# Loading the first batch's q and v by casting transfers from GpSimd's queue

## The chip, the cores and the metric

The kernel runs on one core of one Trainium2 chip. The metric is device time in microseconds (us) of that core, as the median over runs. The engines are named as in the profile: PE (TensorE matmul), PEld (its weight loads), DVE (VectorE), ACT (ScalarE), POOL (GpSimd) and SP (SyncE, which here only issues DMAs).

## What is computed

Four batches, eight heads, 768 tokens, head size 64. The first half is a recurrent retention; the second half mixes its output by a two-dimensional Fourier transform, normalises it and runs a two-layer ReLU network with a residual. Inputs and output are float32.

```python
state = gamma[None, :, None, None] * state + np.einsum('bhd,bhe->bhde', k[:, :, t], v[:, :, t])
y[:, :, t] = scale * np.einsum('bhd,bhde->bhe', q[:, :, t], state)
...
X = np.fft.fft(x, axis=1)
X = np.fft.fft(X, axis=2)
mixed = np.real(X).astype(np.float32)
u = x + mixed
...
ch = np.maximum(un @ w_ch1, 0.0) @ w_ch2
return (u + ch).astype(np.float32)
```

Here `gamma` is one decay per head, `x` is y with the heads side by side (512 wide), and `un` is `u` after its mean and variance are taken out. `w_ch1` is 512 x 2048, `w_ch2` 2048 x 512.

## The kernel before

The recurrence is done in chunks. The 768 tokens are six chunks of 128, and the heads are taken two at a time: four pairs i = 0 to 3, in the order of `PAIR_ORDER`. For each pair the kernel loads q, k and v as float32, casts them to float16 (k with its decay factor, giving `kd`), transposes q and kd on PE, multiplies them chunk by chunk (`wkA`), applies the decay mask on DVE (`atm`), forms the chunk states `wkK` from kd and v, scans them over the chunks on DVE, and adds the part inside a chunk (`atm` times v) and the part from earlier chunks (qT times state) in PSUM (`wkY`). ACT scales the result into the tile `x`. The Fourier transform follows as matmuls with cosine and sine tables (`csp`, `ssp`, `cd`, `sd`) that the kernel itself computes at the start on DVE (`ts_dve`, `td_dve`, lines 288 to 292) and ACT (`t_act`). Then come the two layers (`psh`, line 936 and, for the first half of batch 0, line 953; `psc`, line 979), with the weights cast to float16 by DMAs from POOL (`w1_unit`, line 993, and `w2_unit`, line 1000).

Batch 0 has units of its own, and its order is written out by hand in `first_units`; the function `pin` makes each engine keep exactly the order in which the units issue their instructions. Later batches are merged with the matmuls of the batch before by the times in `LD0`, `TS0` and the like.

These are the units that matter here, all for pair i of batch 0:

- `load_unit(0, i)` issues three loads from SP (line 165), q, k, v for two heads at once, 384 KB each, into buffers of the pool `inp`, which has 11. For q a partition holds six neighbouring tokens (`(p c)`), so a run in memory is 1536 bytes; for k and v it holds every 128th token (`(c p)`), with runs of 256 bytes.
- `q0_unit` (line 398) casts q on POOL into one of two tiles `q16z`, so that pair 2 has to wait until pair 0's was read.
- `k0_unit` (lines 407, 410) casts k on POOL, one instruction per head; for pair 3 ACT does the second head (line 414).
- `v0_unit` (line 423) casts v on POOL into one of four tiles; for pair 3 DVE does half of it (line 427).
- `t0_unit` transposes q (part 0) or kd (part 1) on PE (line 439), and `te_unit` copies the result out of PSUM on ACT (lines 447, 450).
- `am_unit` (line 464) multiplies, `ae_unit` (line 471) masks on DVE, `kv0_unit` (line 486) forms the states, `sc_unit` (line 495) scans, `yi_unit` and `yx_unit` (lines 510, 526) form y, `x0_unit` (line 539) scales it.
- `filler` (line 151) issues matmuls on zeros that nobody reads.
- `half_ids` (lines 351, 353) is two small POOL instructions between the second and the third pair.

On POOL these units stand behind the constants of the start (lines 198 to 347). Batch 1's loads from SP wait for the last but one w2 DMA (`load_unit(1, i, 6)`) and for a matmul of the first layer.

Of the kernel before, what the change touches and what calls it, by code (L numbers as in the profile page):

```python
# [12 lines left out]
ALU = mybir.AluOpType  # L13
f32 = mybir.dt.float32
f16 = mybir.dt.float16
# [3 lines left out]
P = 128  # L19
# [3 lines left out]
NCH = S // P  # L23
# [13 lines left out]
LD0, LD1 = (0.172, 0.226), (-0.370, 0.140)  # L37
HT0 = (0.655, 0.675, 0.673, 0.628)
NPE = 2
ACT_ROWS = ((2, 5, 6, 7, 8, 9, 10, 14), (0, 3, 6, 7, 9, 10, 11, 12, 14, 15), (2, 4, 5, 6, 7, 8, 10, 14))  # L40


@with_exitstack
def kernel(
# [13 lines left out]
    def pool(name, bufs, **kw):  # L58
        return ctx.enter_context(tc.tile_pool(name=name, bufs=bufs, **kw))

    const = pool("const", 1)
    inp = pool("inp", 11)
    vp = pool("vp", 4)
    kp = pool("kp", 3)
    tp = pool("tp", 2)
# [82 lines left out]
    def filler(n):  # L148
        def run():
            for _ in range(n):  # L150
                nc.tensor.matmul(wps, wz[:, 0:P], wz, start=True, stop=True)  # L151
        return run
# [5 lines left out]
    def load_unit(b, i, after=None):  # L158
        def run():
            h0 = 2 * PAIR_ORDER[i]  # L160
            for name, src in srcs.items():
                t = inp.tile([P, 2, NCH, D], f32, tag="in32", name=f"{name}32")
                rows = "h (p c) d -> p h c d" if b < NPE and name == "q" else \
                    "h (c p) d -> p h c d"
                dma = nc.sync.dma_start(t, src[b, h0:h0 + 2].rearrange(rows, p=P))  # L165
                if after is not None:
                    for x in (w_dma[after].ins, lb[0]["mm"].ins):
                        tc.add_manual_dep(dma.ins, x.name,
                                          mybir.DependencyInfo(mybir.DependencyClass.Sync,
                                                               mybir.DependencyReason.DATA),  # L170
                                          reason="loads in turn")
                if b > 1:
                    tc.add_manual_dep(dma.ins, a_of[b - 1, 1].ins.name,
                                      mybir.DependencyInfo(mybir.DependencyClass.Sync,
                                                           mybir.DependencyReason.DATA),
                                      reason="loads behind the transposes")
                in_of[name, b, i] = t
        return run

    for i in range(4):  # L180
        load_unit(0, i)()


    icol_i = const.tile([P, 8], i32, tag="icol_i")
# [44 lines left out]
    def gk_unit(hp):  # L229
        def run():  # L230
            nc.scalar.copy(gk5[:, hp, :, 1:], gk2[:, hp:hp + 1].unsqueeze(1).to_broadcast(
                [P, D, NCH - 2]))
        return run
# [62 lines left out]
    def ts_dve(c):  # L296
        return trig_dve(c, S, KN, icol[:, c:c + 1], icoln[:, c:c + 1])
# [10 lines left out]
    def t_act(idx, part):  # L308
        w = KN if idx < 3 else 257
        r = rs[2 * idx][:, 0:w]  # L310
        ra = rs[2 * idx + 1][:, 0:w]
        sc = float(2.0 * np.pi / (S if idx < 3 else DM))

        def run():
            if part == 0:
                nc.scalar.activation(ra, r, AF.Abs, bias=0.0, scale=1.0)
            elif idx < 3:
                src = (ra, r)[part - 1].rearrange("p (i t) -> p t i", t=2)
                dst = (csp, ssp)[part - 1]
                nc.scalar.activation(dst[:, :, idx, :], src, AF.Sin,  # L320
                                     bias=hpi if part == 1 else 0.0,
                                     scale=-sc if part == 1 else sc)
            else:
                src, dst = (ra, r)[part - 1], (cd16, sd16)[part - 1]
                nc.scalar.activation(dst[:, idx - 3, :], src, AF.Sin,
                                     bias=hpi if part == 1 else 0.0, scale=-sc)
        return run
# [65 lines left out]

    def q0_unit(i):
        def run():
            q16 = q16_of[0, i] = qzs[i % 2].rearrange("p h c d -> p (h c d)")[
                :, 0:NCH * P].rearrange("p (c h d) -> p c h d", c=NCH, h=2)
            nc.gpsimd.tensor_scalar(out=q16, in0=in_of.pop(("q", 0, i)).rearrange(
                "p h c d -> p c h d"), scalar1=1.0, scalar2=1.0, op0=ALU.mult, op1=ALU.mult)
        return run  # L400

    def k0_unit(i):
# [14 lines left out]

    def v0_unit(i):
        def run():
            v32 = in_of.pop(("v", 0, i)).rearrange("p h c d -> p c h d")  # L420
            v16 = v16_of[0, i] = vp.tile([P, NCH, 2, D], f16, tag="v16", name="v16")
            n = NCH if i < 3 else 3
            last_cast[0, i] = nc.gpsimd.tensor_scalar(
                out=v16[:, 0:n], in0=v32[:, 0:n], scalar1=1.0, scalar2=1.0, op0=ALU.mult,
                op1=ALU.mult)
            if n < NCH:
                nc.vector.tensor_copy(v16[:, n:], v32[:, n:])
        return run

    def t0_unit(i, part):  # L430
# [606 lines left out]
    def first_units():  # L1037
        def a(i):
            un = [am_unit(i, 0), am_unit(i, 1)]
            return un  # L1040

        def e(i, *hh):
            return [ae_unit(i, half, h2) for half, h2 in hh]

        def y(i):
            return [yi_unit(i, 0), yi_unit(i, 1)]

        def x(i):
            return [x0_unit(i, 0), x0_unit(i, 1)]

        std = ((0, 0), (0, 1), (1, 0), (1, 1))
        heads = ((0, 0), (1, 0), (0, 1), (1, 1))
        o = PAIR_ORDER
        un = [ts_dve(0), gk_unit(o[0]), gk_unit(o[1]), t_act(0, 0), t_act(0, 1),
              q0_unit(0), t0_unit(0, 0), filler(4), ts_dve(1), te_unit(0, 0), t_act(0, 2),
              k0_unit(0), t0_unit(0, 1), filler(3), te_unit(0, 1), ts_dve(2), td_dve(0), t_act(1, 0),
              t_act(1, 1), t_act(1, 2), v0_unit(0)]
        un += a(0) + [filler(1), kv0_unit(0)] + e(0, *std) + [sc_unit(0)]
        un += [q0_unit(1), t0_unit(1, 0), te_unit(1, 0), t_act(2, 0), t_act(2, 1), filler(4),
               k0_unit(1), t0_unit(1, 1), te_unit(1, 1)]  # L1060
        un += y(0) + [parity_consts, yx_unit(0), filler(2)] + x(0) + [t_act(2, 2), v0_unit(1),
                                                                     half_ids]
        un += a(1) + [csn_unit(0), filler(1), kv0_unit(1)] + e(1, *std) + [sc_unit(1)]
        un += [q0_unit(2), t0_unit(2, 0), te_unit(2, 0), csn_unit(1), filler(3), k0_unit(2),
               t0_unit(2, 1), te_unit(2, 1)]
        un += y(1) + [td_dve(1), yx_unit(1), filler(2)] + x(1) + [
            gk_unit(o[2]), t_act(3, 0), t_act(3, 1), v0_unit(2)]
        un += a(2) + [filler(1), kv0_unit(2)] + e(2, *std) + [sc_unit(2), t_act(3, 2),
                                                              csn_unit(2)]
        un += [q0_unit(3), w1_unit(0), t0_unit(3, 0), te_unit(3, 0), filler(3)] + y(2)  # L1070
        un += [fold_s(0, 0, 258, 0, 1), g0_unit(0, (0,)), k0_unit(3), t0_unit(3, 1),
               te_unit(3, 1), yx_unit(2), gk_unit(o[3]), x0_unit(2, 0), x0_unit(2, 1),
               t_act(4, 0), t_act(4, 1), filler(2), v0_unit(3)]
        un += [w1_unit(g) for g in range(1, 4)] + [w2_unit(g) for g in range(4)]
        un += a(3) + e(3, (0, 0), (1, 0)) + [kv0_unit(3), filler(4), sc_unit(3), t_act(4, 2)]
        un += e(3, (0, 1), (1, 1))
        un += [yx_unit(3), yi_unit(3, 0), x0_unit(3, 0), filler(1), yi_unit(3, 1), x0_unit(3, 1),
               g0_unit(0, (1,)), filler(1)]
        un += [fold_s(0, 0, 130, 1, 2), fold_d(0, 0), s1_unit(0, 0, 0), fold_s(0, 130, 258, 1, 2),
               px_unit(0), fold_d(0, 1, (0,)), xmean_unit(0), fold_d(0, 1, (1,)),  # L1080
               s1_unit(0, 1, 0), s1_unit(0, 0, 1), s1_unit(0, 1, 1), g0_unit(0, (2,)),
               mean_unit(0)]
        un += [s2_unit(0, 0), px_unit(1), s2_unit(0, 1), norm_unit(0, 0), gr_unit(0), gr_unit(1),
               px_unit(2), filler(2), unT_unit(0, 0), xmean_unit(1), mean_unit(1),
               norm_unit(0, 1), s2_unit(0, 2), xmean_unit(2), mean_unit(2), norm_unit(0, 2),
               gr_unit(2), gr_unit(3), edge_zeros, x_edges(1)]
        return un
# [94 lines left out]
```

## Time and profile before

| what | us |
|---|---|
| median of two runs | 247.5 |
| the two runs | 247.04 and 247.95 |
| span of the profiled execution, first to last instruction | 245.4 |
| PE busy | 234.2 |
| DVE busy | 177.0 |
| ACT busy | 124.2 |
| POOL busy | 81.7 |
| first matmul of the first layer (line 953) | starts at 35.08 |
| first matmul of the second layer (line 979) | starts at 48.39 |

The profile gives one execution. Its page lists the span alone, not that execution's time with what lies before the first and behind the last instruction; the two timed runs are 1.6 and 2.6 us above the span. Busy time on PE counts the filler matmuls too. The DMA share is the mean busy share of the core's 16 DMA engines; where two packets overlap on an engine it can go above one.

### The profile page before, as it was taken

Reading aid. Unit: us, or ns where it says so; the run is one execution under the profiler, and the core shown is the slowest. Engines: PE = TensorE matmul, PEld = TensorE weight load, DVE = VectorE, ACT = ScalarE, POOL = GpSimd, SP = SyncE. Lnnn points to the kernel's source line nnn. Section 1 sums busy time; section 2 is a strip of 40 time slices with the busy share of each in tenths; the row PEclk is TensorE's granted clock in tenths of the full one; section 3 lists DMA queues with packets and bytes.
Section 4 is the critical chain, followed back from the end, with each engine's and each line's share of the span. In section 5 each row is a group of like instructions: output and inputs, shape, how many; then the busy total and the mean of one; then the engine's idle time right before and its main releaser. Section 6 shows DMA issues by size and latency. Waiting matters only on the chain.

```text
span 245.4 us, 5309 instructions
## 1 busy us (share of the span) xinstructions
PE 234.2 (95%) x2024; PEld 143.8 (59%) x2024; DVE 177.0 (72%) x430; ACT 124.2 (51%) x276; POOL 81.7 (33%) x146
## 2 busy tenths in 40 slices
PE   6997899999999998999999999999999999999995
PEld 2454668956776655665567546655666455445543
DVE  8997957897897788996885748887895656424112
ACT  8798669587775434751247414742247317202500
POOL 6667601465600057690000646660002405000000
PEclk9999999999999999999999999999999999999999
DMA  8999999699999377999999667786200241221012
GB/s 173 256 260 140 204 195 205 164 245 230 291 229 222 75 168 165 191 181 137 256 272 214 116 141 203 129 120 139 87 1 0 45 151 21 47 85 43 0 45 85
DMA packets 99209, 36.39 MB, mean 148 GB/s; under 512 B 89840, under 2 KB 96240, under 8 KB 99184
## 3 DMA queue, kind: packets, MB, share of 16 engines
q1 hardware_dynamic: 94960, 31.86, 62.2%
q0 software_dynamic: 4224, 4.19, 10.7%
q8 instruction: 16, 0.26, 0.5%
q14 instruction: 9, 0.07, 0.1%
HBM read 27.26 MB, written 6.29 MB: 137 GB/s over the span
## 4 chain that ended last, share of the span: by engine, by line
PE 71%; DMA 7%; DVE 7%; POOL 4%; ACT 4%; SPq 3%; issue 1%; POOLq 0%; ACTq 0%; DVEq 0%
PE psc L979 30%; PE psh L936 25%; DMA k<-in_k_dram 5%; PE ps L736 3%; SPq L165 3%; PE wkA L600 3%; DMA q<-in_q_dram 2%; PE wkY L654 2%; PE pq L833 2%; PE wkY L650 1%; POOL u L870 1%; PE wkK L619 1%; ACT un L885 1%; DVE bst L889 1%; POOL kd L407 1%
## 5 line engine op out<-in xcount | busy, mean ns | idle before, releaser
L979 PE MATMUL psc<-w,ht 128*128 128x512 f16 (+2 forms) x400 | 89.3, 371 | 0.0
L936 PE MATMUL psh<-unT,w 128*128 128x384 f16 x448 | 81.6, 326 | 0.4 <-ACT ht L940 0.2
L979 PEld LDWEIGHTS <-ht 128*128 128x128 f16 x400 | 37.5, 98 | 36.5 <-issue 0.2
L936 PEld LDWEIGHTS <-w 128*128 128x128 f16 x448 | 42.3, 98 | 24.7 <-issue 1.4
L940 ACT ACTIVATE ht<-psh 128x384 f16<-128x384 f32 x64 | 30.9, 489 | 41.7 <-PE psh L936 41.1
L870 POOL TENSOR_TENSOR u<-u,x 128x256 f32<-128x256 f32 x21 | 13.3, 635 | 100.3 <-DVE u L840 91.0
L983 DVE SCALAR_TENSOR_TENSOR ob<-psc,stats,u 128x512 f32<-128x512 f32 (+2 forms) x25 | 18.1, 726 | 26.1 <-PE psc L979 26.0
L942 DVE TENSOR_SCALAR ht<-psh 128x384 f16<-128x384 f32 x48 | 26.2, 548 | 7.7 <-PE psh L936 7.4
L603 DVE TENSOR_TENSOR atm<-wkA,maskp 128x512 f16<-128x512 f32 x36 | 23.8, 681 | 1.6 <-PE wkA L600 1.6
L891 ACT ACTIVATE un<-u,stats 128x512 f16<-128x512 f32 x21 | 15.2, 722 | 16.7 <-DVE stats L890 12.1
L889 DVE BATCH_NORM_STATS2 bst<-u 128x6 f32<-128x512 f32 x21 | 14.6, 694 | 7.7 <-POOL u L872 7.6
L629 DVE SCALAR_TENSOR_TENSOR s<-s,gk,wkK 128x128 f16<-128x128 f16 x48 | 16.3, 341 | 3.7 <-ACT s L625 2.7
L662 ACT ACTIVATE x<-wkY,gexp 128x384 f16<-128x384 f32 x24 | 12.8, 581 | 8.0 <-PE wkY L654 8.0
L151 PE MATMUL wps<-ht 128*128 128x512 f16 x40 | 13.5, 444 | 2.2 <-POOL ht L202 2.2
L383 POOL TENSOR_SCALAR kd<-k,gexp 128x384 f16<-128x384 f32 x24 | 13.8, 585 | 3.6 <-DMA k<-in_k_dram 3.6
L872 POOL TENSOR_TENSOR u<-u,x 128x256 f32<-128x256 f32 x21 | 13.3, 635 | 3.0 <-DVE stats L890 3.0
L600 PE MATMUL wkA<-qTz,kT 128*128 128x256 f16 x72 | 13.4, 273 | 0.1
L835 ACT COPY qn<-pq 128x128 f32<-128x128 f32 x18 | 4.9, 272 | 13.6 <-PE pq L833 13.6
L953 PE MATMUL psh<-unT,w 128*128 128x128 f16 x192 | 11.5, 219 | 0.1
L953 PEld LDWEIGHTS <-w 128*128 128x128 f16 x192 | 11.0, 98 | 0.7 <-issue 0.5
L840 DVE SCALAR_TENSOR_TENSOR u<-pq,g,qn 128x256 f32<-128x256 f32 x18 | 8.5, 472 | 3.3 <-PE psh L936 2.5
L388 POOL TENSOR_SCALAR v<-v 128x768 f16<-128x768 f32 x12 | 10.0, 831 | 1.3 <-DMA v<-in_v_dram 1.3
(164 smaller groups left out, 315.6 us busy)
## 6 DMA issues: line engine op xcount, KB each, us to landing
q<-in_q_dram SPq DMA_DIRECT2D x16, 384.0 KB, 6.3
k<-in_k_dram SPq DMA_DIRECT2D x16, 384.0 KB, 5.6
v<-in_v_dram SPq DMA_DIRECT2D x16, 384.0 KB, 6.3
out_dram<-ob SPq DMA_DIRECT2D x23, 256.0 KB, 2.6
w<-in_moe_w_ch_dram POOLq DMA_DIRECT2D x8, 512.0 KB, 10.8
unT<-un SPq DMA_TRANSPOSE x15, 2.4
out_dram<-ob SPq DMA_DIRECT2D x1, 192.0 KB, 1.9
qTz<-q16z SPq DMA_TRANSPOSE x8, 3.9
```

Of the source, the lines that this page charges most:

```text
L600: mm = nc.tensor.matmul(wk[:, c2], st["kT"][:, c, :], st["qT"][:, :, c, :], start=True, stop=True)
L603: nc.vector.tensor_tensor(out=st["atm"][:, 2 * part:2 * part + 2], in0=wk, in1=maskp[:, PAIR_ORDER[i]].unsqueeze(1).to_broadcast([P, 2, 2, ...
L629: nc.vector.scalar_tensor_tensor(out=s16[:, c], in0=s16[:, c - 1], scalar=gk2[:, hp:hp + 1], in1=wk[:, c - c0], op0=ALU.mult, op1=ALU.add)
L870: nc.gpsimd.tensor_tensor(out=u[:, kb, 0:256], in0=u[:, kb, 0:256], in1=x[:, kb, 0, 1:257], op=ALU.add)
L889: nc.vector.bn_stats(bst, u[:, kb, :])
L891: una = nc.scalar.activation(un, u[:, kb, :], AF.Identity, bias=stats[:, kb, 0:1], scale=-1.0)
L936: nc.tensor.matmul(psh, w116[:, cb, fb * P:(fb + 1) * P], unT[:, cb, rt * 384:(rt + 1) * 384], start=(cb == 0), stop=(cb == 3))
L940: nc.scalar.activation(ht16[:, fb, :], psh, AF.Relu, bias=0.0, scale=-1.0)
L942: nc.vector.tensor_scalar(out=ht16[:, fb, :], in0=psh, scalar1=-1.0, scalar2=0.0, op0=ALU.mult, op1=ALU.max)
L953: mm = nc.tensor.matmul(psh[:, f], w116[:, cb, fb * P:(fb + 1) * P], unT[:, cb, kb * P:(kb + 1) * P], start=(cb == 0), stop=(cb == 3))
L979: nc.tensor.matmul(psc[:, c0:c1], ht16[:, fb, rb3 * P:(rb3 + 1) * P], w216[:, fb, c0:c1], start=(fb == 0), stop=(fb == NFB - 1))
L983: nc.vector.scalar_tensor_tensor(out=ob[:, c0:c1], in0=psc[:, c0:c1], scalar=lb[b]["st"][:, rb, 3:4], in1=lb[b]["u"][:, rb, c0:c1], op0=AL ...
```

## The change

For batch 0 only k is still loaded from SP, for all four pairs (`HW0`, `load0`). q and v are loaded by DMAs on POOL's queue that read float32 and write float16 at once into the tile that the transposes and matmuls read, one DMA per head. So the casts of q and v fall away, on POOL and, for pair 3, on DVE. q gets four tiles of its own (`q0p`), and `inp` goes from 11 buffers to 9. The DMAs are issued ahead: q and v of pair 0 and q of pair 1 stand behind the constants; v of pair 1 stands where v of pair 0 was cast, and so on. The k casts and all orders of PE and ACT stay. Batches 1 to 3 are loaded and cast as before.

```diff
-    inp = pool("inp", 11)
+    inp = pool("inp", 9)
+    q0p = pool("q0p", 4)
...
+    def load0(name, i):
+        h0 = 2 * PAIR_ORDER[i]
+        t = in_of[name, 0, i] = inp.tile([P, 2, NCH, D], f32, tag="in32", name=f"{name}32")
+        rows = "h (p c) d -> p h c d" if name == "q" else "h (c p) d -> p h c d"
+        nc.sync.dma_start(t, srcs[name][0, h0:h0 + 2].rearrange(rows, p=P))
+
     for i in range(4):
-        load_unit(0, i)()
+        for name in HW0:
+            load0(name, i)
...
     def q0_unit(i):
         def run():
-            q16 = q16_of[0, i] = qzs[i % 2].rearrange("p h c d -> p (h c d)")[
-                :, 0:NCH * P].rearrange("p (c h d) -> p c h d", c=NCH, h=2)
-            nc.gpsimd.tensor_scalar(out=q16, in0=in_of.pop(("q", 0, i)).rearrange(
-                "p h c d -> p c h d"), scalar1=1.0, scalar2=1.0, op0=ALU.mult, op1=ALU.mult)
+            h0 = 2 * PAIR_ORDER[i]
+            q16 = q16_of[0, i] = q0p.tile([P, NCH, 2, D], f16, tag="q0", name="q0")
+            for h2 in range(2):
+                nc.gpsimd.dma_start(q16[:, :, h2, :],
+                                    q[0, h0 + h2].rearrange("(p c) d -> p c d", p=P))
...
     def v0_unit(i):
         def run():
-            v32 = in_of.pop(("v", 0, i)).rearrange("p h c d -> p c h d")
+            h0 = 2 * PAIR_ORDER[i]
             v16 = v16_of[0, i] = vp.tile([P, NCH, 2, D], f16, tag="v16", name="v16")
-            n = NCH if i < 3 else 3
-            last_cast[0, i] = nc.gpsimd.tensor_scalar(
-                out=v16[:, 0:n], in0=v32[:, 0:n], scalar1=1.0, scalar2=1.0, op0=ALU.mult,
-                op1=ALU.mult)
-            if n < NCH:
-                nc.vector.tensor_copy(v16[:, n:], v32[:, n:])
+            for h2 in range(2):
+                last_cast[0, i] = nc.gpsimd.dma_start(
+                    v16[:, :, h2, :], v[0, h0 + h2].rearrange("(c p) d -> p c d", p=P))
...
-        un = [ts_dve(0), gk_unit(o[0]), gk_unit(o[1]), t_act(0, 0), t_act(0, 1),
-              q0_unit(0), t0_unit(0, 0), filler(4), ts_dve(1), te_unit(0, 0), t_act(0, 2),
+        un = [q0_unit(0), v0_unit(0), q0_unit(1), ts_dve(0), gk_unit(o[0]), gk_unit(o[1]), t_act(0, 0), t_act(0, 1),
+              t0_unit(0, 0), filler(4), ts_dve(1), te_unit(0, 0), t_act(0, 2),
               k0_unit(0), t0_unit(0, 1), filler(3), te_unit(0, 1), ts_dve(2), td_dve(0), t_act(1, 0),
-              t_act(1, 1), t_act(1, 2), v0_unit(0)]
+              t_act(1, 1), t_act(1, 2), v0_unit(1)]
...
-        un += [q0_unit(1), t0_unit(1, 0), te_unit(1, 0), t_act(2, 0), t_act(2, 1), filler(4),
+        un += [q0_unit(2), t0_unit(1, 0), te_unit(1, 0), t_act(2, 0), t_act(2, 1), filler(4),
...
-        un += [q0_unit(3), w1_unit(0), t0_unit(3, 0), te_unit(3, 0), filler(3)] + y(2)
+        un += [w1_unit(0), t0_unit(3, 0), te_unit(3, 0), filler(3)] + y(2)
```

More of the change, by code (lines that the diff above doesn't have):

```diff
@@ L39 @@
 NPE = 2
+HW0 = ("k",)
 ACT_ROWS = ((2, 5, 6, 7, 8, 9, 10, 14), (0, 3, 6, 7, 9, 10, 11, 12, 14, 15), (2, 4, 5, 6, 7, 8, 10, 14))
@@ L1058, in first_units @@
         un += a(0) + [filler(1), kv0_unit(0)] + e(0, *std) + [sc_unit(0)]
-        un += [q0_unit(1), t0_unit(1, 0), te_unit(1, 0), t_act(2, 0), t_act(2, 1), filler(4),
+        un += [q0_unit(2), t0_unit(1, 0), te_unit(1, 0), t_act(2, 0), t_act(2, 1), filler(4),
                k0_unit(1), t0_unit(1, 1), te_unit(1, 1)]
-        un += y(0) + [parity_consts, yx_unit(0), filler(2)] + x(0) + [t_act(2, 2), v0_unit(1),
+        un += y(0) + [parity_consts, yx_unit(0), filler(2)] + x(0) + [t_act(2, 2), v0_unit(2),
@@ L1062, in first_units @@
                                                                      half_ids]
         un += a(1) + [csn_unit(0), filler(1), kv0_unit(1)] + e(1, *std) + [sc_unit(1)]
-        un += [q0_unit(2), t0_unit(2, 0), te_unit(2, 0), csn_unit(1), filler(3), k0_unit(2),
+        un += [q0_unit(3), t0_unit(2, 0), te_unit(2, 0), csn_unit(1), filler(3), k0_unit(2),
                t0_unit(2, 1), te_unit(2, 1)]
         un += y(1) + [td_dve(1), yx_unit(1), filler(2)] + x(1) + [
-            gk_unit(o[2]), t_act(3, 0), t_act(3, 1), v0_unit(2)]
+            gk_unit(o[2]), t_act(3, 0), t_act(3, 1), v0_unit(3)]
@@ L1068, in first_units @@
         un += a(2) + [filler(1), kv0_unit(2)] + e(2, *std) + [sc_unit(2), t_act(3, 2),
                                                               csn_unit(2)]
-        un += [q0_unit(3), w1_unit(0), t0_unit(3, 0), te_unit(3, 0), filler(3)] + y(2)
+        un += [w1_unit(0), t0_unit(3, 0), te_unit(3, 0), filler(3)] + y(2)
         un += [fold_s(0, 0, 258, 0, 1), g0_unit(0, (0,)), k0_unit(3), t0_unit(3, 1),
                te_unit(3, 1), yx_unit(2), gk_unit(o[3]), x0_unit(2, 0), x0_unit(2, 1),
-               t_act(4, 0), t_act(4, 1), filler(2), v0_unit(3)]
+               t_act(4, 0), t_act(4, 1), filler(2)]
```

## The prediction

> **What bounds the kernel now.** I read the page first. PE is busy 95% of the span, so after the start-up the kernel is TensorE-bound; the idle slices of PE lie in the first six.
>
> ```profile
> PE   6997899999999998999999999999999999999995
> PEclk9999999999999999999999999999999999999999
> DMA  8999999699999377999999667786200241221012
> ```
>
> Each digit is a fortieth of the span, 6.1 us. The clock is full throughout. DMA is full from the start, and that is what the first slices wait for. So I read the chain of waits from 0 to 45 us in order of time:
>
> ```profile
> 2.69 2.26 SPq L165
> 7.08 2.48 SPq L165
> 9.61 5.65 DMA k<-in_k_dram
> 15.34 0.59 POOL kd L407
> ...
> 19.64 0.83 POOL q16z L398
> 20.47 0.90 POOL w L993
> 21.41 1.28 POOL kd L407
> ...
> 24.55 0.60 DVE atm L471 x2
> ...
> 28.41 0.69 PE ps L736 x6
> ```
>
> The four head pairs of batch 0 come in through SP's queue until 15.3, then GpSimd's (POOL's) casts of the third and fourth k carry the chain, then the attention of the fourth pair, then the first mixing step. From 61 us on the chain is nearly all matmuls. So the change acts on the front, and what it does to the front reaches the end: in the stretches table PE is busy 13.62 of 14 us from 34 to 48, 12.70 of 13 from 48 to 61, so at most 0.3 us can be won back there.
>
> What paces the front is the transfers. The DMA view of one pair's stretch, 7.08 to 11.66 us, in 40 slices:
>
> ```profile
> GB/s 255 255 376 376 362 362 358 309 277 284 291 286 282 255 233 224 219 217 217 212 219 210 224 215 215 224 215 221 219 219 217 217 217 217 217 226 235 300 242 215
> ```
>
> q, in runs of 1536 bytes, moves at about 370 GB/s; k and v, in runs of 256, at 217. A load of 0.393 MB is 1.06 us for q, 1.81 for k or v, 4.7 us a pair, and the waits of the four k casts stand at that pace.
>
> POOL's own timeline gives the prices:
>
> ```profile
> 3.98 0.14 POOL L347 MEMSET x<- 128x48 f16 x1
> 4.18 0.83 POOL L398 TENSOR_SCALAR q16z<-q 128x768 f16<-128x768 f32 x1
> 6.07 0.60 POOL L407 TENSOR_SCALAR kd<-k,gexp 128x384 f16<-128x384 f32 x1 [1.05 <-DMA k<-in_k_dram]
> ...
> 20.41 0.96 POOL L993 DMA_DIRECT2D w<-in_moe_w_ch_dram  x1
> 21.41 1.27 POOL L407 TENSOR_SCALAR kd<-k,gexp 128x384 f16<-128x384 f32 x1
> 22.66 0.50 POOL L423 TENSOR_SCALAR v<-v 128x384 f16<-128x384 f32 x1
> 23.12 2.29 POOL L993 DMA_DIRECT2D w<-in_moe_w_ch_dram  x3
> 25.38 2.99 POOL L1000 DMA_DIRECT2D w<-in_moe_w_ch_dram  x4
> ```
>
> A cast is 0.83 us. A casting DMA holds POOL too: eight took 0.96 + 2.29 + 2.99 = 6.24 us, 0.78 each, for 512 runs each.
>
> **The change, part by part.**
>
> Removed on POOL: four q casts and four v casts, 7 x 0.83 + 0.50 = 6.3 us; on DVE half a v cast, 0.54 us at 23.10, followed by 0.92 us of idle, so worth nothing. On SP eight loads go; the four k are issued by about 3 us. From the last byte to the release is about 2 us: the first w1 DMA took 5.6 from issue to landing, 0.96 of it issue and 1.05 MB at the 410 GB/s read in the w stretch, 2.6, transfer. So the last k is in by about 1.4 + 4 x 1.81 + 2 = 11 us, and no k cast waits for data any more.
>
> Added on POOL: 16 casting DMAs, one per head, of 128 x 6 = 768 runs of 64 elements. Call the price d. No row shows one of 768 runs. If the price is fixed, d is 0.78; if it goes by runs, 0.78 x 768/512 = 1.17. Some of it must be fixed, so I take a little under the middle, 0.95, and keep both ends.
>
> Moved: the first transfers of q and v. SP issued q at 0.81; POOL comes to its first DMA only after its constants, at 3.98 + 0.14 = 4.12. By the built order of the changed kernel POOL then does q0, v0, q1 (six DMAs), kd(0), v1, q2 (four), kd(1), v2 (two), the two small half-identities, q3 (two), kd(2), v3 (two), one w1 DMA, kd(3). So kd(2) stands behind 14 DMAs, the three k casts (1.25 + 1.15 + 1.15 from their rows) and the half-identities (13.17 to 13.73, 0.56): it ends at 4.12 + 4.11 + 14d = 8.23 + 14d, which is 21.5 at d = 0.95. Before it ended at 16.49.
>
> Behind kd(2) queue the transposes of k, and ScalarE, whose order is unchanged: kT copy, x of pair 1, the table work, qT of pair 3, its half of kd(3). In the rows of ScalarE this ran almost without a gap, from 17.09 to 22.38; without its 0.15 us gap it ends 5.74 us after kd(2). POOL's half of kd(3) ended 0.30 later, at 22.68, and the mask product of pair 3 on DVE started at 24.55. With ScalarE alone as its limit it starts 0.45 us sooner, 7.61 us after kd(2). In the changed kernel POOL's half is out at 21.5 + 2 x 0.95 + 0.96 + 1.27 = 25.6, before ScalarE's at 21.5 + 5.7 = 27.3, so ScalarE is the limit: shift = 8.23 + 14d + 7.61 - 24.55 = 14d - 8.7. That is 4.6 us at d = 0.95, 2.2 at 0.78, 7.7 at 1.17.
>
> Transfers of q and v: now 768 runs of 256 bytes read and 128 written. No row shows such packets. At the price of a 256-byte run a head costs 1.81 / 2 = 0.91 us; by its written bytes alone, at the 205 GB/s of the w stretch, 0.098 MB is 0.48. I take 0.91, the nearest row for short runs; it is just below d, so transfers land some 3 to 4 us behind their issue, and the orders above leave that much everywhere (v3, issued by 23.4, is needed near 29). The upper end, twice the price for half the run written, is a rival.
>
> [...]
>
> w: w1's last three and w2 start at about 25.6 against 23.12, 2.5 later. The first use of w1, at 34.8, shifts by 4.6. Batch 1's loads, which wait in SP for w2, shift by 2.5, less than PE's work: hidden, and worth up to the 0.3 us of PE idle. The input pool has 9 buffers for 11, so the last pair's loads of batches 2 and 3 go behind transposes on SP; their casts come at 107.95 and 160.86 us, about 10 us after the new issue: nothing, with a bound of 0.8 us, since two issues of about 1.6 us then go into 2.5 us of SP idle ahead of the transposes at 151.83.
>
> Sum: 245.4 + 4.6 - 0.3 = 249.7 us of span. The page gives a span alone; the median of the two runs shown, 247.5, is 2.1 above it, and I add that: **251.8 us**.
>
> **A rule against the change.** Row first: the DVE scalar op of line 290 takes 0.36 us alone at 2.93, but 0.86 at 4.37, beside POOL's q cast: the two block each other, and there DVE lost. The Trainium skill, SBUF — State Buffer, section "SBUF: two separate sides", says that such a DVE op locks GpSimd out of the shared port, so that descriptors of its DMAs cannot be written meanwhile. The trace agrees that they exclude each other; no run here shows a casting DMA losing. By the rule the sum would be that of rival 2; by the row it stays.
>
> **The rivals.**
> 1. Price by runs, d = 1.17: shift 7.7, 255 us. For it: six runs per partition instead of four. Against: three DMAs in a row at 0.76 leave room for a fixed part.
> 2. DVE goes first: lines 288 and 290 run between 4.1 and 8.8 for 0.2 + 0.36 + 0.42 + 0.36 + 0.34 + 0.3 = 2.0 us of their unblocked time. If POOL's first six DMAs stand still for it, everything behind shifts by 2.0: 253.8 us.
> 3. Transfers become the bound: at 1.81 us a head, 4 x 1.81 + 16 x 1.81 = 36.2 us from 1.4, plus 2 to land, v3 is in at about 40 instead of the 29 needed: some 11 more, 262 us. For it only that no row has 128-byte writes.
> 4. The shift does not reach the end: if the 2.5 us by which w and batch 1's loads move is what counts, 250.
> 5. Faster: POOL's issue is much cheaper than the w rows, place kd(2). Below d = 8.7/14 = 0.62 the mask product of pair 3 starts sooner than before. At 0.45, ScalarE permitting, 2.4 us sooner: 245 us. Against it: eight rows at 0.75 to 0.96.
>
> **How the numbers follow.** Chances: forecast (d from 0.78 to 1.05, 249.4 to 253.2 us) 0.49; rival 1 0.18; rival 2 0.14; rival 3 0.05; rival 4 0.07; rival 5 0.07. The range 247.5 to 256.0 holds the forecast and rivals 1, 2, 4 and leaves out 3 and 5, 0.12, and some of rival 1's tail. About 2% is what a measurement of this kernel can tell from no change: below 242.5 is faster, above 252.5 slower. Faster needs d near 0.25: 0.02. Slower: rivals 1, 2, 3 (0.37) and the forecast's upper end from d = 1.0, 0.09: 0.46. Within 2%: 0.52.
>
> **What would show it.** Right: POOL's DMA rows at 0.8 to 1.05 us back to back from 4.1; kd(2) ending near 21.5; no wait of POOL for k; the mask product of pair 3 near 29; the first mixing matmul, at 28.41 before, near 33; from 48 us on the same rows, later by 4 to 5. Wrong: DMA rows far from 0.95 (rivals 1, 5), long rows only while DVE runs lines 288 and 290 (rival 2), transposes waiting for q or v rather than kd (rival 3), or a shift that shrinks between 33 and 61 us (rival 4).

## The result and the profile after

The changed kernel takes 254.25 us, median of two runs (253.92 and 254.58), against 247.5 (247.04 and 247.95): a ratio of 1.0291, 95% interval 1.0257 to 1.0325. It is slower, and the time lies in the range given. The forecast of 251.8 was 2.45 us too low, and most of its explanation of the loss was wrong, as the trace shows. The ratios here and below leave out an execution that took over 1.5% longer than the fastest of its kernel; there was one, 256.8 us in run 6.

The profiled execution took 253.92 us with a span of 252.1, so 1.8 lie outside the span. The span grew by 6.7 us. The page's strips, 40 slices of 6.3 us each:

```profile
PE   4199889999999998999999999999999999999994
...
PEclk9779999999999999999999999999999999999999
DMA  8999999289999914998899359989100141221012
```

PE is busy 15% of the second slice (6.3 to 12.6 us), where the strip before showed a 9, and the granted clock falls to 0.7 in the second and third. From the fourth slice on the strip reads much as before. The chain of waits (start, length, what) names what PE waits for:

```profile
4.12 0.51 POOL q L408
...
5.15 6.36 DMA q<-in_q_dram
11.65 0.80 PE tq L446 x6
```

The chain now begins with the transfer of the first q. The prediction's chain through the third k cast is gone. PE's own timeline (start, length, line, operation, and in brackets the idle time before it and what ended it), after:

```profile
11.65 0.80 PE L446 MATMUL tq<-ident,q 128*128 128x128 f16 x6 [6.75 <-DMA q<-in_q_dram]
12.24 1.91 PE L153 MATMUL wps<-ht 128*128 128x512 f16 x4
13.95 0.85 PE L446 MATMUL tq<-ident,kd 128*128 128x128 f16 x6
...
15.88 0.51 PE L471 MATMUL wkA<-qTz,kT 64*128 64x128 f16 x12
...
20.22 0.51 PE L471 MATMUL wkA<-qTz,kT 64*128 64x128 f16 x12
...
22.38 0.50 PE L446 MATMUL tq<-ident,kd 128*128 128x128 f16 x6
...
24.33 0.51 PE L471 MATMUL wkA<-qTz,kT 64*128 64x128 f16 x12
...
28.25 0.49 PE L446 MATMUL tq<-ident,kd 128*128 128x128 f16 x6 [1.25 <-ACT kd L424]
...
29.68 0.51 PE L471 MATMUL wkA<-qTz,kT 64*128 64x128 f16 x12
...
33.91 0.69 PE L743 MATMUL ps<-csp,eo 128*128 128x193 f16 x6 [0.41 <-DVE eo L696]
```

and the same rows of the kernel before, where the first mixing matmul came at 28.41:

```profile
5.07 0.82 PE L439 MATMUL tq<-ident,q16z 128*128 128x128 f16 x6 [0.17 <-POOL q16z L398]
5.68 1.91 PE L151 MATMUL wps<-ht 128*128 128x512 f16 x4
...
8.95 0.51 PE L464 MATMUL wkA<-qTz,kT 64*128 64x128 f16 x12 [0.24 <-ACT kT L450]
```

The first q transposes start 6.58 us later, the first product `wkA` 6.93. Then the shift shrinks: the products of the later pairs started at 13.67, 18.34 and 24.18 before, so the gaps between the four are 4.34, 4.11 and 5.35 us for 4.72, 4.67 and 5.84, so 1.43 us come back, and 5.50 remain at the first mixing matmul. The new pace is a loop between PE and DVE. DVE's rows of the second pair:

```profile
20.60 1.95 DVE L478 SCALAR_TENSOR_TENSOR atm<-wkA,maskf 128x384 f16<-128x384 f32 x4 [0.38 <-PE wkA L471]
22.47 0.81 DVE L502 TENSOR_TENSOR_SCAN s<-gk,wkK 128x320 f16<-128x320 f32 x1
```

The product starts at 20.22, the mask takes 1.95, the scan 0.81, then PE does `yx` (0.53, at 23.33) and two fillers (0.60), and the next product starts at 24.33: 4.11 us. The last gap is longer than this loop: there PE waits 1.25 us for ScalarE's half of the last k (line 424, in the row at 28.25). Transfers no longer set the pace of a pair; but the loop began 6.9 us late, and the three gaps together win back only 1.43 us of it.

GpSimd's timeline answers the disputed prices:

```profile
4.06 2.06 POOL L408 DMA_DIRECT2D q<-in_q_dram  x2
6.11 1.67 POOL L433 DMA_DIRECT2D v<-in_v_dram  x2
7.73 1.71 POOL L408 DMA_DIRECT2D q<-in_q_dram  x2
9.48 0.59 POOL L417 TENSOR_SCALAR kd<-k,gexp 128x384 f16<-128x384 f32 x1
...
19.54 0.60 POOL L420 TENSOR_SCALAR kd<-k,gexp 128x384 f16<-128x384 f32 x1
```

A casting DMA of 768 runs takes 0.82 to 0.86 us, the first two 1.03 each on average. The first k cast runs at 9.48, in time; PE did not need it before q.

Why q lands so late is in the DMA view. Packets finished on the two queues in stretches of 2 us (a head of q is 768 packets, a pair 1536; each reads 256 bytes):

| us | SyncE's queue, after | GpSimd's queue, after | SyncE's, k held back | GpSimd's, k held back |
|---|---|---|---|---|
| 5.5 to 7.5 | 1360 | 512 | none | 946 |
| 7.5 to 9.5 | 1290 | 279 | none | 1834 |
| 9.5 to 11.5 | 240 | 2114 | 619 | 1139 |
| 11.5 to 13.5 | none | 2441 | 1202 | 759 |

The last two columns are the second experiment below. From 5.5 to 9.5, while SyncE's k loads are in flight, GpSimd's queue finishes 791 of 3441 packets, 23%; when they are done it does 2100 to 2400 in 2 us. So the first q, issued by 6.1, is in at 11.5. The 23% is a mean and no steady share: in stretches of half a microsecond GpSimd's queue has none before 6.5, 439 of 567 packets from 7.0 to 7.5, and 35 of 1128 from 8.0 to 9.5. The Trainium skill, DMA: Bandwidth & Descriptors, section "Queues, rings and completion order", says that each DMA engine takes turns between the queues it has work for, a packet of several descriptors at a time. The trace agrees that the engines serve both queues in the same microseconds; how long a turn is it does not show, and the packets finished are far from equal here, 77 to 23.

The late part of the kernel gives the rest. DVE's rows stand 5.65 us later than before up to 163.7 (in the time of the kernel before) and 6.43 from 170.3. The chain of waits between:

```profile
158.19 5.96 DMA qTz<-q16z
...
167.72 4.33 DMA kT<-kd
```

Before, no piece of the chain from 147 to 170 is a DMA. With nine buffers in the input pool SyncE issues three loads there (153.18, 154.64, 157.70) among the transposes, where one stood before (147.53), and the transpose behind them comes 0.7 us later than the shift alone explains (158.19 against 151.83). PE then waits 0.5 us for `kT`, the only such wait in the trace.

### The profile page after: what moved, and what is told of

Its sections match the earlier page's. It is cut to its first block, busy times and chain, and to the rows that moved or that the text cites. A ratio compares the mean times of both kernels' runs of the same rounds, so it can differ in the third digit from the quotient of the medians.

```text
span 252.1 us, 5304 instructions
## 1 busy us (share of the span) xinstructions
PE 234.9 (93%) x2024; PEld 144.3 (57%) x2024; DVE 174.8 (69%) x429; ACT 123.8 (49%) x276; POOL 87.8 (35%) x154
## 3 DMA queue, kind: packets, MB, share of 16 engines
q0 software_dynamic: 16768, 5.77, 20.2%
## 4 chain that ended last, share of the span: by engine, by line
PE 66%; DMA 11%; ACT 6%; DVE 6%; POOL 6%; issue 2%; SPq 1%; POOLq 0%; ACTq 0%
PE psc L986 28%; PE psh L943 21%; PE ps L743 3%; DMA k<-in_k_dram 3%; DMA q<-in_q_dram 3%; PE wkA L607 2%; DMA qTz<-q16z 2%; DMA v<-in_v_dram 2%; DMA kT<-kd 2%; PE psh L960 1%; PE wps L153 1%; PE wkY L661 1%; PE pq L840 1%; POOL kd L392 1%; SPq L167 1%
## 5 line engine op out<-in xcount | busy, mean ns | idle before, releaser
L478 DVE SCALAR_TENSOR_TENSOR atm<-wkA,maskf 128x384 f16<-128x384 f32 x16 | 7.9, 550 | 9.4 <-PE wkA L471 9.4
L960 PE MATMUL psh<-unT,w 128*128 128x128 f16 x192 | 11.5, 219 | 0.1
L842 ACT COPY qn<-pq 128x128 f32<-128x128 f32 x18 | 4.9, 272 | 13.6 <-PE pq L840 13.5
```

The source lines that it names most:

```text
L960: mm = nc.tensor.matmul(psh[:, f], w116[:, cb, fb * P:(fb + 1) * P], unT[:, cb, kb * P:(kb + 1) * P], start=(cb == 0), stop=(cb == 3))
```

## The experiments

The expectations call A the theory that the transfers on GpSimd's queue land late, the first q above all, and that everything behind follows from that. The rivals against it are that ScalarE or GpSimd's own row of instructions sets the front (the prediction's own reason), that it is a matter of when q is issued and not of what moves beside it, and that the buffers or the later batches carry the loss. Each run is compared with runs of the kernel before on the same chip, which there took 246.58 to 247.24 us.

### 1. ScalarE's tables ahead

```diff
-              t0_unit(0, 0), filler(4), ts_dve(1), te_unit(0, 0), t_act(0, 2),
-              k0_unit(0), t0_unit(0, 1), filler(3), te_unit(0, 1), ts_dve(2), td_dve(0), t_act(1, 0),
...
+              ts_dve(1), t_act(1, 0), t_act(1, 1), t_act(1, 2), ts_dve(2), td_dve(0), t_act(2, 0),
+              t_act(2, 1), t_act(2, 2), csn_unit(0), csn_unit(1), t0_unit(0, 0), filler(4), te_unit(0, 0),
```

> The changed kernel with one thing moved: ScalarE computes the tables of the first three column groups (lines of t_act 0 to 2 and two of csn) before it copies the first transposed q, and not after. Theory A: the first q lands late (11.5 us) and ScalarE, whose table work stands behind its copy, idles 6.5 us and then paces the front; with some 5 us of its work done in that gap, the first mixing matmul comes at 30 to 31.5 us for 33.9, and the time is 250.5 to 252. Theory B, that of the prediction: the POOL queue up to the third k cast sets the front; then nothing changes, 33.9 us and 254.

Measured 254.04 us, ratio 1.0283 (1.0259 to 1.0307): as the changed kernel, so A's forecast failed here and B's number came. ScalarE's timeline in this kernel:

```profile
12.55 0.80 ACT L454 COPY qTz<-tq 128x768 f16<-128x768 f16 x1 [2.08 <-PE tq L446]
14.90 0.80 ACT L457 COPY kT<-tq 128x768 f16<-128x768 f16 x1 [1.55 <-PE tq L446]
17.60 0.80 ACT L454 COPY qTz<-tq 128x768 f16<-128x768 f16 x1 [1.90 <-PE tq L446]
```

ScalarE now waits for PE ahead of its first three copies, 1.55 to 2.08 us each time, and still the products start at 15.89, 20.08, 24.19 and 29.53 and the mixing at 33.76, 0.15 sooner. In the changed kernel ScalarE runs without a gap from 17.59 to 28.1 and the chain passes through it; this run shows that the part of it that was moved, up to the third pair, was full and yet not the limit. The wait of 1.25 us for ScalarE's half of the last k is the same here (28.11): that part was not moved. B's number is not B's reason either: the third k cast ends at 20.14, and the transposes that read it start at 22.38 (22.24 here) without a wait. So the prediction's path through kd(2) falls, and of ScalarE's only the last pair's wait is left.

### 2. k behind the first q

```diff
-    for i in range(4):
-        for name in HW0:
-            load0(name, i)
+    load0("k", 0)
...
+    def rest_k():
+        for i in range(1, 4):
+            x = load0("k", i)
+            tc.add_manual_dep(x.ins, q_dma[1].ins.name,
...
+        un = [q0_unit(0), rest_k, v0_unit(0), q0_unit(1), ts_dve(0), gk_unit(o[0]), gk_unit(o[1]), t_act(0, 0), t_act(0, 1),
```

> The changed kernel with the loads of k for pairs 1 to 3 held back until the first q has landed. Theory A1: the four k loads, 1.57 MB issued ahead, keep the DMA engines until 9.5 us and q waits behind them; then q lands at about 8 us, the first transposes start at 8 to 8.5 for 11.65, and the time is 251 to 252.5. Theory A2: q is late by itself (issued at 4.06, two issues of 1.0, short packets, fixed latency); then the first transposes stay at 11 or later, 254. Theory B: no change, 254, whenever q lands.

Measured 253.51 us, ratio 1.025 (1.0207 to 1.0293), where A1 gave 251 to 252.5. The four executions run from 252.04 to 254.19, and the trace is of the fastest; what follows rests on the rows, since the time alone does not stand clear of the changed kernel's. The first ten microseconds in the DMA view, after:

```profile
q1 hardware_dynamic: 6196, 1.57, 91.7%
q0 software_dynamic: 1085, 0.14, 21.4%
```

and with k held back (columns: packets, MB, share of the 16 engines' time):

```profile
q0 software_dynamic: 3201, 0.40, 63.2%
q1 hardware_dynamic: 1552, 0.39, 17.2%
```

and PE:

```profile
9.15 0.80 PE L453 MATMUL tq<-ident,q 128*128 128x128 f16 x6 [4.25 <-DMA q<-in_q_dram]
```

q, issued at the same time, lands at 9.0 instead of 11.5: 2.9 us behind its last issue instead of 5.4. So 2.5 us of the 6.6 come from the k loads that move beside it, and 4.1 remain with no load of SyncE's beside it. k of the second pair is now late (GpSimd waits 0.87 us for it and casts it at 14.76 instead of 13.92), and the mixing comes at 32.38, only 1.5 sooner.

### 3. Only v by casting transfers

```diff
-HW0 = ("k",)
+HW0 = ("q", "k")
```

with q cast on GpSimd as before, into its own four tiles.

> Half of the change: q and k from SP's queue, q cast on POOL as before, only v by casting transfers. Theory A: q is in by 4 us, ScalarE does not idle, and the front costs nothing: the first mixing matmul at 27.5 to 29 us (28.4 before), 246.5 to 249 us, with up to 0.8 of it from the 9 buffers. Theory B: the third k cast ends at 4.12 + 4.11 + 3 x 0.83 + 6 x 0.85 = 15.8 us, before it was 16.5: the same forecast. If the short transfers themselves were the trouble, wherever they stand, it stays above 252.

Measured 253.01 us, ratio 1.0226 (1.0191 to 1.0262): a miss, since A expected v to do little harm. The first q transposes are back at 5.07. GpSimd and PE:

```profile
4.96 1.87 POOL L431 DMA_DIRECT2D v<-in_v_dram  x2
7.02 0.82 POOL L406 TENSOR_SCALAR q<-q 128x768 f16<-128x768 f32 x1 [0.19 <-DMA q<-in_q_dram]
7.84 0.86 POOL L415 TENSOR_SCALAR kd<-k,gexp 128x384 f16<-128x384 f32 x1
```

```profile
9.35 0.51 PE L444 MATMUL tq<-ident,kd 128*128 128x128 f16 x6 [2.15 <-POOL kd L418]
...
10.75 0.82 PE L469 MATMUL wkA<-qTz,kT 64*128 64x128 f16 x12
...
12.90 0.69 PE L491 MATMUL wkK<-v,kd 128*64 128x64 f16 x9 [0.54 <-DMA v<-in_v_dram]
```

Two things, both of the pair ahead: v's DMAs and the next q's cast stand on GpSimd ahead of the first k cast, which comes at 7.84 for 6.07; and v itself, issued by 6.8, is in at 12.9, six microseconds later, beside SyncE's q and k. The mixing is at 31.82, 3.4 late. Whichever of the two is moved to GpSimd's queue arrives five to six microseconds after its issue. The span is 5.9 longer, so 2.5 more are lost in later batches: PE waits 0.68 us at 65.87, 0.94 at 114.64 and 0.41 at 171.35. Nine buffers alone (next run) do not explain that much, and it stays open.

### 4. The kernel before with nine buffers

```diff
-    inp = pool("inp", 11)
+    inp = pool("inp", 9)
```

> The kernel before with 9 input buffers for 11 and nothing else. Theory C: the last 0.8 us of the loss come from the buffers, because the last pair's loads of batch 3 are then issued among the transposes on SP's queue: 248.0 to 248.6 us, and the shift appears behind 160 us in the trace. If the loss is from the front alone: 247.5.

Measured 248.23 us against 247.05, ratio 1.0038 (1.0022 to 1.0054): 0.9 us by the ratio, as forecast. In the trace, which is of one of the fastest executions (247.34), DVE's rows step later by 0.4 us between 109 and 113 and by 0.3 between 166 and 170, so the loss does not stand behind 160 us alone.

### 5. The first q issued at 1.56 instead of 4.06

```diff
+    q_first = q0p.tile([P, NCH, 2, D], f16, tag="q0", name="q0")
+    for h2 in range(2):
+        nc.gpsimd.dma_start(q_first[:, :, h2, :],
+                            q[0, 2 * PAIR_ORDER[0] + h2].rearrange("(p c) d -> p c d", p=P))
```

behind the first iotas, ahead of all other constants; `q0_unit(0)` only takes the tile.

> The changed kernel with the first pair's two q DMAs issued right after POOL's iotas, at 1.6 us for 4.06; the four k loads stay ahead in SP's queue. Theory A1: POOL's transfers get next to nothing of the DMA engines while SP's queue has packets, so q still lands at 9.5 to 11 and the time is 252.5 to 254. Rival A2: the late issue is what costs, so q lands by 6 to 7, the first transposes start there, and with the first k cast at 9.5 to 10.7 the mask product of pair 0 starts near 13.5 for 16.3: 250.5 to 251.5.

Measured 251.23 us, ratio 1.0163 (1.0143 to 1.0182).

```profile
8.13 0.50 PE L453 MATMUL tq<-ident,q 128*128 128x128 f16 x6 [1.29 <-DMA q<-in_q_dram]
...
10.79 0.77 PE L453 MATMUL tq<-ident,kd 128*128 128x128 f16 x6 [1.30 <-POOL kd L427]
```

Issued 2.5 us sooner, q is used 3.5 sooner, and still 4.7 us after its last issue (3.43); with k held back (next run) it is in by 6.64. The time is A2's, and A1's reason is too strong: from 5.5 to 6.5 GpSimd's queue finishes 1143 of 1194 packets although SyncE's loads are not done. After that the first k cast is the limit: it stands on GpSimd behind six DMAs and the displaced constants and comes at 9.59. The mixing is at 31.64, 3.2 late for 5.5. Of the single edits to the changed kernel this one saves most. That does not weigh q's issue against what moves beside it, as run 2 also makes k late.

### 6. Both: q early, and k behind it

To the diff of run 5 comes, behind the two early DMAs:

```diff
+    for i in range(1, 4):
+        tc.add_manual_dep(load0("k", i).ins, q_dma.ins.name,
```

> The same, and the loads of k for pairs 1 to 3 held back until q has landed. Theory A1: only now does the early issue help: q lands at 5 to 6, and the limit is the first k cast on POOL behind six DMAs (ends at 10.6): mask product of pair 0 near 13, mixing at 31 to 31.5, 250.5 to 251.5. If A2 is right it is the same as early_q or later, because k now comes late.

Measured 252.06, 252.57 and 255.28 us, ratio 1.0249 (1.0201 to 1.0297), and 256.8 in a fourth execution (median of all four 253.93); A1's 250.5 to 251.5 was missed. The trace is of the execution at 255.28, with the mixing at 35.71.

```profile
6.64 0.85 PE L457 MATMUL tq<-ident,q 128*128 128x128 f16 x6
...
10.80 0.51 PE L457 MATMUL tq<-ident,kd 128*128 128x128 f16 x6 [2.00 <-POOL kd L431]
...
16.95 0.80 PE L457 MATMUL tq<-ident,q 128*128 128x128 f16 x6 [2.71 <-DMA q<-in_q_dram]
```

The first q is in time for 6.64, and now q of the second pair, issued by 9.6, meets the k loads that were held back, and PE waits 2.71 us for it, 7.4 after its issue. In this execution holding SyncE's loads back only changes which transfer on GpSimd's queue is the late one; the two faster ones have no trace.

### 7. The changed kernel with eleven buffers

```diff
-    inp = pool("inp", 9)
-    q0p = pool("q0p", 4)
+    inp = pool("inp", 11)
```

with q in the two tiles `q16z` of the kernel before.

> The changed kernel with 11 input buffers; there is room for them because q is written into the two tiles of the kernel before and not into four of its own. Theory C: the loss behind 160 us (0.75 us) goes: 252.8 to 253.4. If the buffers cost nothing: 254 or more, since q of pairs 2 and 3 may now have to wait for a tile.

Measured 252.81 us, ratio 1.0233 (1.021 to 1.0256). The mixing is at 33.78, 5.4 late, and from 164 us to the last output the shift of DVE's rows stays between 5.19 and 5.20: the step is gone. The span is 251.0, 1.1 less than the changed kernel's. So 0.8 (the step) to 1.1 us (the span) of the 6.7 is the buffers, which agrees with run 4's 0.9. The tiles of q changed with them: one pair of q transfers (12.81) waits 0.52 us for its tile, which holds up no transpose. By that the third k cast ends at 20.66 instead of 20.14, and the mixing is not later for it, which speaks once more against the path through kd(2).

### 8. v of the later pairs only

From the kernel before: the first pair untouched; v of pairs 1 to 3 by casting DMAs, eleven buffers, the last pair's q and k loaded behind v of pair 1.

```diff
+    for name, i in (("q", 0), ("k", 0), ("v", 0), ("q", 1), ("k", 1), ("q", 2), ("k", 2)):
+        load0(name, i)
...
-              t_act(1, 1), t_act(1, 2), v0_unit(0)]
+              t_act(1, 1), t_act(1, 2), v0_unit(0), v0_unit(1), rest_loads]
```

> From the kernel before: pair 0 untouched; v of pairs 1 to 3 by casting transfers, one pair ahead; q and k by SP and casts, those of the last pair held back until v of pair 1 has landed; 11 buffers. Theory A1 with a loop of 4.15 us per pair (product 0.46, mask 1.95, scan 0.8, y 0.5, fillers 0.6 one after the other): with pair 0 in time, the four products start at 9, 13.2 to 13.6, 17.5 to 18 and 23, for 8.95, 13.67, 18.34 and 24.18 before: 246 us, ratio 0.994 to 0.998. If casting transfers cost wherever they stand: 249 or more.

Measured 247.47 us against 247.24, ratio 1.0016 (0.9998 to 1.0035): no difference, and the gain that was forecast did not come.

```profile
11.50 0.51 PE L455 MATMUL tq<-ident,q16z 128*128 128x128 f16 x6 [1.32 <-POOL q16z L412]
...
14.68 0.51 PE L480 MATMUL wkA<-qTz,kT 64*128 64x128 f16 x12
```

The casting transfers themselves do no harm where the first pair does not wait for one. But v's two DMAs (1.87 us) stand on GpSimd ahead of the second pair's q cast and take a microsecond there, which the loop's 4.10 us for the next pair and a shorter last gap give back (products at 18.78 and 24.14, for 18.34 and 24.18). In the last gap, 5.36 us, PE waits 1.17 for ScalarE's half of the last k, as in the changed kernel.

### 9. v of the last two pairs only

From the kernel before: all else by SyncE, casts as before; v of pairs 2 and 3 by casting DMAs behind the k casts of pairs 1 and 2.

```diff
+    for i in range(4):
+        for name in ("qkv" if i < 2 else "qk"):
+            load0(name, i)
...
-        un += y(0) + [parity_consts, yx_unit(0), filler(2)] + x(0) + [t_act(2, 2), v0_unit(1),
+        un += y(0) + [parity_consts, yx_unit(0), filler(2)] + x(0) + [t_act(2, 2), v0_unit(2), v0_unit(1),
```

> From the kernel before, with eleven buffers: q and k of all pairs and v of the first two pairs come by SyncE and are cast as before; only v of the third and fourth pairs comes by casting DMAs, issued behind the k casts of the second and third pairs. Theory A (a transfer on GpSimd's queue lands late beside SyncE's loads; harmless where nobody waits for it for 6 us): SyncE's stream is 0.79 MB shorter and ends near 17 instead of 20; first products of the pairs near 8.9, 13.7, 18.0, 22.3, first mixing matmul near 26.5 (28.41 before), time 245.2 to 246.2. Theory B (the front is bound by the bytes and runs of the transfers, whoever issues them): all data in no sooner, mixing 28 to 29, time 247 to 248.

Measured 247.53 us against 246.58, ratio 1.0034 (1.0021 to 1.0047): a hair slower, where A expected 245.2 to 246.2. The mixing comes at 28.54, so the numbers are those of theory B.

```profile
15.89 0.51 PE L448 MATMUL tq<-ident,q16z 128*128 128x128 f16 x6 [0.85 <-POOL q16z L405]
...
20.28 0.66 PE L495 MATMUL wkK<-v,kd 128*64 128x64 f16 x10 [0.63 <-DMA v<-in_v_dram]
...
22.88 0.49 PE L448 MATMUL tq<-ident,kd 128*128 128x128 f16 x6 [0.50 <-ACT kd L421]
```

v of the third pair, issued by 13.65, is in at 20.2: 6.6 us, even longer than in the changed kernel, as SyncE's q and k of the last pairs move beside it. The DMAs and both casts fill GpSimd almost without a gap from 10.7 us on, so q of the third pair is cast 0.85 too late for PE. B's reason, that all data are in no sooner, is not what the rows show: from 18 to 20 us SyncE's queue finishes 58 packets, where it had 1732 before. But nobody gains by that, as PE waits for GpSimd's cast, for v and for ScalarE's half of the last k.

### 10. Only q by casting transfers

```diff
-HW0 = ("k",)
+HW0 = ("k", "v")
```

with v cast on GpSimd as before.

> The changed kernel with v brought back to SyncE's queue and GpSimd's cast; only q comes by casting DMAs. Theory A (q of the first pair is the late transfer, because it is issued last and shares with SyncE's loads): SyncE now has eight loads of short runs, 14.5 us of transfers, in flight beside q, so the first q transposes come at 11.5 or later (11.65 in the changed kernel, 5.07 before), q of the second pair is late too, first mixing matmul at 34 or later, time 254 to 259. Theory B (v is what costs, q is harmless): first transposes near 6, time 248 to 250.

Measured 255.2 us against 246.58, ratio 1.0355 (1.0338 to 1.0372).

```profile
11.57 0.80 PE L445 MATMUL tq<-ident,q 128*128 128x128 f16 x6 [6.68 <-DMA q<-in_q_dram]
...
33.96 0.69 PE L742 MATMUL ps<-csp,eo 128*128 128x193 f16 x6 [0.40 <-DVE eo L695]
```

The front is that of the changed kernel to 0.1 us, although v is back with SyncE. So q alone is enough for the whole loss of the front; v, which costs 3.4 us by itself, is hidden behind it, and the two do not add. One part of the expectation failed: q of the second pair was not late (its transposes at 17.09, no wait). The span is 7.8 longer, 2.2 of it after the mixing: PE waits 0.47 us at 115.63 and 1.33 at 154.32, the second time for a transpose on SyncE's queue. Why is as open as in run 3.

## Why the prediction was right and wrong

Right: the direction, and that the change acts on the front and reaches the end undiminished. From the first mixing matmul to 163.7 us the shift of the main rows stays between 5.5 and 5.7. That the time lies in the range, and that 4.6 us of shift came near the 5.5 measured, is luck: the range was drawn around prices on GpSimd and one path behind them, and that path did not set the time.

**The price of a casting DMA.** 0.95 was taken between 0.78 and 1.17; it is 0.85, so rival 1 falls. Of that some 0.64 is fixed, an estimate from the rows of 512 and of 768 runs, 0.78 and 0.85, as if the rest went by runs. The formula held: kd(2) ends at 8.23 + 14 x 0.85 = 20.1, and the trace has 20.14. With this price the sum would have given a shift of 14 x 0.85 - 8.7 = 3.2 us; 5.5 were measured. So the path through kd(2) and ScalarE was not the longest one: the transposes start 2.2 us after kd(2) without a wait, and run 1, which empties ScalarE up to the third pair, changes nothing.

**The step that failed** is the sentence that transfers of q and v "land some 3 to 4 us behind their issue, and the orders above leave that much everywhere". Both halves are wrong for the first pair. They landed 5.4 us behind, because the price of 1.81 / 2 = 0.91 us a head took the DMA engines to be free for them. Alone they are even cheaper: 2441 packets in 2 us are 0.63 us a head. Beside SyncE's four k loads they got a quarter of the packets from 5.5 to 9.5, and none before 6.5. And the orders left nothing: PE's second piece of work is the transposes of the first q, at 5.07 before, and the two DMAs of q are issued from 4.06 to 6.12. The prediction itself had "POOL comes to its first DMA only after its constants, at 4.12" and set that against kd(2) alone, not against PE's first row. 4.12 + 2 x 0.95 + 3, its own numbers, would have put the transposes at 9 and said that the first pair starts 4 us late. Behind q stands a second delay of the first pair: in run 5, with q there by 8.1, PE waits for the first k cast, which stands on GpSimd behind six DMAs, and 3.2 us of loss are left at the mixing. That is the kind of path that the prediction added up, but at the first pair and not at the third.

The prediction counted it as a gain that k is in by 11. But that k comes in sooner is 2.5 us of why q comes in later (run 2), and k was not needed before q.

**Rival 2** (DVE goes first): the first two DMAs took 2.06 us instead of 1.7, so 0.4 us and not 2.0. In runs 3, 5, 8 and 9 the first two on the queue took 1.87 wherever they stood (4.96, 1.56, 8.70, 11.78), so DVE's part is at most 0.2. **Rival 3** (transfers become the bound) had its sign come true, as the transposes wait for q, but for another reason: not slow packets, but shared engines and only until 9.5 us. **Rival 4** (the shift does not reach the end) falls. It had batch 1's loads move by 2.5; they moved by 5.5 (50.35 for 44.89).

**w** did not move: its last three w1 DMAs start at 23.09 for 23.12, not 25.6, as the DMAs ahead are 0.1 us cheaper each, the first w1 DMA took 0.78 instead of 0.96, and GpSimd's half of kd(3) 0.62 instead of 1.27. Nothing hung on it.

**The 0.3 us to be won back** did not come: over the same stretches the shift grows from 5.50 to 5.66.

**Nine buffers** were costed at "nothing, with a bound of 0.8 us", and the step between 163.7 and 170.3 is 0.78; run 7, without it, is 1.1 us of span shorter. The two issues did not fit into SP's idle: with the load that was there before and two output DMAs they fill SP from 153.2 to 158.1.

From 251.8 to 254.25: front 5.5 for 4.6 (0.9), nothing won back (0.3) and a little more lost (0.2), buffers 0.8, the rest of the span 0.2 (6.7 less the steps named). That is 2.4.

**The clock.** PE stood still for 6.75 us, and the next rows ran on a lower granted clock. The stretches 6 to 12 and 12 to 18 us (length, busy time and count of PE, PEld, DVE, ACT, POOL, granted clock, DMA share, GB/s):

```profile
6.00:12.00 6.00, 0.35 (x4) 0.39 (x5) 2.65 (x5) 0.00 (x0) 5.96 (x9) 0.74 1.86 177
12.00:18.00 6.00, 6.00 (x50) 3.18 (x48) 1.66 (x4) 3.98 (x7) 5.96 (x10) 0.69 1.77 112
```

Six transposes took 0.80 and 0.85 where they take 0.51 later, four fillers 1.91 for 1.03. Most of this the kernel before pays too: its first transposes took 0.82 and its next four fillers 1.91, though its profile grants the full clock there (1.00 from 0 to 12 us). From the first transposes to the first product it needs 3.88 us, the changed kernel 4.23, so of the 6.93 us by which the first product is late only 0.35 arise here. What a full clock would have saved no run shows. The Trainium skill, TensorE: Matmul & The Clock Gate, section "Part 1: The HAM clock gate", has PE's clock fall to half after an idle window of about 3.4 us. The trace agrees in kind, with 0.69 as the mean of a stretch that holds slow and full parts; but as rows just as slow stand at 1.00 in the kernel before, the granted clock alone does not prove it. The prediction had no term for it, since it saw no idle PE.

What stays open: why v alone and q alone lose another 2.2 to 2.5 us in later batches, more than nine buffers cost the kernel before (neither was run with eleven buffers); and what decides which queue's packets move when both have work. No version measured beats the kernel before.

## What to carry to other kernels

Before moving a load to another queue, find the first row of the engine that consumes it and ask three things: when the new queue's engine is free to issue, how long a transfer takes from issue to landing, and what else is in flight then. A busy engine that gets its data a few microseconds later pays the delay once, at the start, and later slack gives back only what the next loop leaves, here 1.4 of 6.9 us. A transfer that moves beside a long stream from another queue should be priced by a delay measured beside such a stream, not by its own size; here 5.4 to 7.4 us from issue to use instead of 2.9 to landing.

## What the runs showed of the hardware

Casting transfers from 256-byte runs to 128-byte runs are not slow by themselves: 2441 packets in 2 us, 312 GB/s read, more than the 217 GB/s at which plain copies of the same runs moved in the kernel before. Beside SyncE's loads they got 23% of the packets over 4 us (791 of 3441), in bursts: within half a microsecond anything from none to 439 of 567. A casting DMA of 768 runs held GpSimd for 0.85 us where one of 512 runs took 0.78, so the price grew by a tenth for half as many runs again.
